# A top-k attention, SwiGLU and expert kernel: the last 64 keys' values padded with zeros to 128 rows, the queries transposed raw

## The chip, the cores and the metric

The kernel runs on one core of a Trainium2 chip. The metric is the device time of one execution in microseconds. The kernel before was timed three times: 1239.47, 1242.8 and 1243.44 us, so the median is 1242.8 us. The execution with the profile took 1240.91 us, of which the span from the first to the last instruction is 1239.3 us.

TensorE is PE in the profile (PEld is its weight load), VectorE is DVE, ScalarE is ACT, GpSimd is POOL, and SyncE, which only issues transfers here, is SP.

## The reference

Three layers follow each other. Only the first one is touched by the change.

```python
B, H, S, D = 4, 8, 576, 64                       # attention
scores = scale * np.matmul(q, k.transpose(0, 1, 3, 2))
kth = np.partition(scores, -32, axis=-1)[..., -32:-31]
scores = np.where(scores >= kth, scores, -1e9)   # keep the 32 largest of 576
attn = softmax(scores)
x = np.matmul(attn, v)                           # -> 2304 tokens x 512
...
xn = x / rms(x) * rms_g                          # SwiGLU, 512 -> 1536 -> 512
x = (silu(xn @ w_gate) * (xn @ w_val)) @ w_out
...
e_idx = argmax(x @ w_gate2 + bias[modality])     # one of 8 experts per token
out[t] = gate[t] * (relu(x[t] @ w1[e]) @ w2[e])
```

## The kernel before

**Tiles and steps.** For each batch and head there are 576 queries and 576 keys, that is 4 chunks of 128 and a rest of 64. A tile is 128 queries against all 576 keys. `tiles` lists 144 of them; two tiles make one of 72 steps. A main step has one chunk `c` of the two heads of a pair `p` (in batch 2, for the first two chunks, two chunks of one head). A remainder step has two tiles, each with the 64 last queries of head 0 above the 64 last queries of head 1 of one pair.

**One tile's way through the engines.** `dma_q` loads a step's queries six steps ahead. `split_q` (POOL, four steps ahead) makes two halves of them, `hi` (rounded to the short fp32r form) and `lo = q - hi`, each written twice side by side. `trans_q` (two steps ahead) transposes the four 128x128 blocks on PE (L465), and ACT copies the result to `qS` (L473, L478). `qk` multiplies them with the keys (L530). ACT copies the scores out (L543), and DVE finds the 32nd largest score of each row: two folded halves (L545 to L547), then four MAX8 and three MATCH_REPLACE8 for each tile (L565, L568), eight MAX8 on L565 for a step. ACT and POOL then make the softmax (L595, L599, L603), `tr` transposes it on PE (L625, L630) into `pT` (four chunks of keys) and `pr` (the last 64 keys; those of a step's even tile stand on partitions 0 to 63, those of the odd tile on 64 to 127). `av` multiplies both with the values (L671): per chunk of keys three products of fp16 halves, so 12 matmuls with 128 rows from `pT` and 3 with 64 rows from `pr`. `dma_v` loads the last 64 values twice, to both halves of the partitions, so that either half of `pr` finds them. Batch 0, heads 0 to 3, is done in fp32 instead of fp16 halves (`whole`).

**The second layer inside the first.** When the heads of one or two blocks of 128 tokens are done, they form a granule, and its SwiGLU (L729 to L750 on PE, u on L772, router logits on L809) is put into the attention steps in small atoms with a budget for each seventh of a step (`mlp_slot`). What is left after step 71 runs alone. The experts follow (L1161 to L1243).

**What sets the order.** The code is written in the order of `step`, but each engine's list of instructions is put in order by a scheduler before the launch, which goes by its own estimate of when operands are there. The order is fixed then: an engine runs its list from first to last and waits where an operand is late.

**Start.** `w_out` comes in twelve transfers on SP's queue into space of the other weights and is turned from float64 to fp16 halves by DVE (L279, L284, L288), ACT and POOL (L297); the first keys and queries are loaded between them.

Of the kernel before, what the change touches and what calls it, by code (L numbers as in the profile page):

```python
# [8 lines left out]
F32 = mybir.dt.float32  # L9
# [11 lines left out]
def topk_attention_swiglu_moe_kernel(  # L21
# [50 lines left out]

    NMB = B * CM
# [4 lines left out]
    def main_steps(b, cs):  # L78
        for p in range(NP):
            if len(cs) == 2:  # L80
                for hh in range(2):
                    steps.append([(b, p, hh, c) for c in cs])
            else:
                steps.append([(b, p, hh, cs[0]) for hh in range(2)])
        granules.append((len(steps) - 1, [b * CM + c for c in cs]))

    def rem_steps(b):
        for p in range(0, NP, 2):
            steps.append([(b, p, None, None), (b, p + 1, None, None)])
        if b % 2:  # L90
            granules.append((len(steps) - 1, [NMB + b // 2]))

# [121 lines left out]
    def front(exact):  # L214
# [218 lines left out]

        def dma_q(s):
            qr = ap_.tile([128, 2, D], F32, name="qr", tag="qr", bufs=QB)
            t0, t1 = steps[s]
            b, p, hh, c = t0
            if hh is not None and t1[2] == hh:
                src = q[b, 2 * p + hh, 0:SM, :].rearrange("(p c) d -> p c d", c=CM)
                nc.sync.dma_start(out=qr, in_=src[:, c:c + 2, :])  # L440
            else:
                for t, (b, p, hh, c) in enumerate(steps[s]):
                    if hh is not None:
                        src = q[b, 2 * p + hh, 0:SM, :].rearrange("(p c) d -> p c d", c=CM)
                        nc.sync.dma_start(out=qr[:, t, :], in_=src[:, c, :])
                    else:
                        for i in range(2):
                            nc.sync.dma_start(out=qr[i * SR:(i + 1) * SR, t, :], in_=q[b, 2 * p + i, SM:S, :])
            raw["q", s] = qr

        def split_q(s):
            qr = raw.pop(("q", s))
            qs = ap_.tile([128, 2, 2, 2, D], F32R, name="qs", tag="qs", bufs=2)
            z = zero.unsqueeze(2).unsqueeze(3).to_broadcast([128, 2, 2, D])
            q2 = qr.unsqueeze(2).to_broadcast([128, 2, 2, D])
            nc.gpsimd.tensor_tensor(out=qs[:, :, 0], in0=q2, in1=z, op=OP.add)
            nc.gpsimd.tensor_tensor(out=qs[:, :, 1], in0=q2, in1=qs[:, :, 0].bitcast(F32), op=OP.subtract)
            raw["qs", s] = qs

        def trans_q(s):  # L460
            qs = raw.pop(("qs", s))
            pt = ps_m.tile([128, 512], F32R, name="pq", tag="sm")
            for t in range(2):
                for j in range(2):
                    nc.tensor.transpose(  # L465
                        pt[:, (2 * t + j) * 128:(2 * t + j + 1) * 128],
                        qs[:, t, j].rearrange("p a d -> p (a d)"),
                        identr,
                    )
            src = pt.bitcast(F32)  # L470
# [883 lines left out]
```

## Time and profile before

| | PE | DVE | ACT | POOL | granted PE clock | MAX8 of L565 |
|---|---|---|---|---|---|---|
| whole span, 1239.3 us | 1138.8 | 928.2 | 830.5 | 731.2 | 0.94 | 576 |
| 61 to 205 us | 102.06 | 143.96 | 115.85 | 100.93 | 0.65 | 104 |
| 237 to 281 us | 41.51 | 23.62 | 30.43 | 26.38 | 0.88 | 16 |
| 281 to 824 us | 537.45 | 524.87 | 451.95 | 416.84 | 1.00 | 408 |
| 824 to 905 us | 79.10 | 17.48 | 30.55 | 33.40 | 1.00 | 0 |

All numbers are of the profiled execution (1240.91 us, span 1239.3 us); engine columns are busy microseconds, the clock is a share of full speed (1.00 is 2.4 GHz, 0.50 is 1.2 GHz). Attention steps run from about 21 to 824 us. From 824 to 905 us the rest of the SwiGLU runs, from there on the experts. A matmul's busy time reaches to its modelled end, which lies some 0.2 us behind the moment at which the next one can start; what a matmul costs is therefore read from start to start.

### The profile page before, as it was taken

What the parts mean: (1) busy time and instruction counts of PE and PEld (TensorE: products, weight loads), DVE (VectorE), ACT (ScalarE), POOL (GpSimd) and SP (SyncE); (2) the same over time, 40 slices, a digit from 0 to 9 for tenths busy, and PEclk for the clock granted to TensorE, in tenths of its full rate; (3) what the DMA queues carried; (4) which work ended last, traced back from release to release, by engine and by line L of the source; (5) the groups of instructions that cost most, each with busy time, mean ns of one, the idle gap of its engine ahead of it and who ended that gap; (6) DMA issues with size and microseconds to landing.
All of it is one profiled execution on the core that took longest, in us unless ns stands there. A gap on an engine that the chain in (4) does not pass through costs nothing. (4 is left out here: it accounts for less than half of the span.)

```text
span 1239.3 us, 32187 instructions
## 1 busy us (share of the span) xinstructions
PE 1138.8 (92%) x12286; PEld 1039.9 (84%) x12286; DVE 928.2 (75%) x2886; ACT 830.5 (67%) x1757; POOL 731.2 (59%) x843
## 2 busy tenths in 40 slices
PE   6976677999999999999999999999997999999994
PEld 6965566888999989999998999999986898798883
DVE  8999999759999999998999999971125526244161
ACT  6868888777888888878888887873333435344260
POOL 7866766858767879867889676564434312222100
PEclk9865676989999999999999999999997999999997
DMA  8242312011000111000011000013006726354230
GB/s 295 51 129 82 100 44 82 13 45 39 21 17 9 32 41 47 24 13 15 17 38 40 28 17 2 11 32 124 11 19 193 247 70 230 128 173 149 66 113 20
DMA packets 69624, 87.54 MB, mean 71 GB/s; under 512 B 34626, under 2 KB 43974, under 8 KB 69448
## 3 DMA queue, kind: packets, MB, share of 16 engines
q1 hardware_dynamic: 62360, 67.86, 17.9%
q0 software_dynamic: 5424, 13.16, 3.3%
q10 hardware_dynamic: 1664, 4.19, 0.9%
q8 instruction: 107, 1.75, 0.6%
q14 instruction: 69, 0.57, 0.2%
HBM read 75.58 MB, written 10.92 MB: 70 GB/s over the span
## 5 line engine op out<-in xcount | busy, mean ns | idle before, releaser
L565 DVE MAX8 w<-w 128x8 f32<-128x296 f32 x576 | 251.9, 462 | 1.2
L599 POOL TENSOR_TENSOR s<-s,r 128x576 f32<-128x576 f32 x144 | 201.1, 1417 | 31.3 <-ACT r L595 31.1
L568 DVE MATCH_REPLACE8 w<-w 128x296 f32<-128x296 f32 x432 | 194.9, 455 | 0.0
L750 PE MATMUL pf<-xT,wg 128*128 128x128 f16 (+1 forms) x2448 | 172.0, 224 | 4.2 <-DVE T L879 2.6
L750 PE MATMUL pf<-xT,wv 128*128 128x128 f16 (+1 forms) x2448 | 167.7, 222 | 0.0
L750 PE MATMUL po<-wo,h 128*128 128x264 f16 (+1 forms) x1296 | 157.4, 275 | 0.9 <-ACT t L777 0.9
L530 PE MATMUL ps<-kS,qS 128*128 128x288 f32 x640 | 138.6, 346 | 20.7 <-DVE w L546 19.6
L750 PEld LDWEIGHTS <-wg 128*128 128x128 f16 x2448 | 148.3, 99 | 11.1 <-issue 4.9
L750 PEld LDWEIGHTS <-wv 128*128 128x128 f16 x2448 | 145.3, 98 | 4.3
L750 PEld LDWEIGHTS <-h 128*128 128x128 f16 x1296 | 122.0, 98 | 18.8 <-issue 1.4
L1137 DVE TENSOR_TENSOR wl<-wr,wh 128x1024 fp32r<-128x1024 f32 x64 | 76.7, 1220 | 66.1 <-ACT wh L1136 66.1
L530 PEld LDWEIGHTS ps<-kS,qS 128*128 128x128 f32 x640 | 104.0, 215 | 23.8 <-ACT r L595 14.9
L603 ACT ACTIVATE s<-s,mbs 128x576 f32<-128x576 f32 x144 | 113.3, 789 | 14.2 <-POOL s L599 13.9
L595 ACT ACTIVATE r<-s,mbs 128x576 f32<-128x576 f32 x144 | 105.0, 781 | 15.1 <-POOL mbs L586 15.0
L625 PE MATMUL pt<-identr,s 128*128 128x128 f32 x576 | 97.6, 300 | 16.9 <-ACT s L603 16.1
L543 ACT COPY s<-ps 128x576 f32<-128x576 f32 x144 | 93.1, 646 | 22.1 <-PE ps L530 21.5
L1243 POOL DMA_INDIRECT out_dram<-o,idx x23 | 23.2, 1010 | 138.0 <-ACT o L1242 106.9
L1184 PE MATMUL ph<-xh,wh 128*128 128x256 f32 x352 | 99.7, 287 | 1.0 <-PEq L1301 1.0
L1184 PE MATMUL ph<-xl,wh 128*128 128x256 f32 x352 | 98.5, 282 | 0.0
L1184 PE MATMUL ph<-xh,wl 128*128 128x256 f32 x352 | 97.1, 284 | 0.8 <-issue 0.8
L782 POOL TENSOR_TENSOR t<-u,t 128x512 f32<-128x512 f32 x54 | 69.6, 1289 | 47.9 <-ACT t L777 30.3
L671 PE MATMUL pt<-vs,pT 128*128 128x64 f16 (+1 forms) x1680 | 88.4, 198 | 8.7 <-POOL pT L639 6.7
(205 smaller groups left out, 2779.0 us busy)
## 6 DMA issues: line engine op xcount, KB each, us to landing
wr<-in_moe_w_dram SPq DMA_DIRECT2D x56, 512.0 KB
wst<-in_moe_w_gate_dram SPq DMA_DIRECT2D x24, 256.0 KB
wst<-in_moe_w_val_dram SPq DMA_DIRECT2D x24, 256.0 KB
kr<-in_k_dram SPq DMA_DIRECT2D x32, 128.0 KB
vt<-in_v_dram SPq DMA_DIRECT2D x32, 128.0 KB
x_d<-xo SPq DMA_DIRECT2D x16, 256.0 KB
wr<-in_moe_w_dram ACTq DMA_DIRECT2D x8, 512.0 KB
qr<-in_q_dram SPq DMA_DIRECT2D x112, 32.0 KB
```

Of the source, the lines that this page charges most:

```text
L530: nc.tensor.matmul(out=ps[:, a, 0:HS], lhsT=qS[i // 2][:, i % 2, j, o2:o2 + 128], rhs=kt[:, m, ks], start=(n == 0), stop=(n == len(ops) - 1),)
L543: nc.scalar.copy(out=s.rearrange("p (a k) -> p a k", a=2), in_=ps[:, :, 0:HS])
L565: steps.append(lambda: dve.max(lists[t][:, 8 * r:8 * r + 8], src[t] if r == 0 else dst[t]))
L568: steps.append(lambda: dve.match_replace(out=dst[t], in_to_replace=lists[t][:, 8 * r:8 * r + 8], in_values=src[t] if r == 0 else dst[t], i ...
L595: nc.scalar.activation(out=d["r"], in_=d["s"], func=AF.Relu, scale=-BIG, bias=d["mb"][:, 1:2])
L599: nc.gpsimd.tensor_tensor(out=d["s"], in0=d["s"], in1=d.pop("r"), op=OP.subtract)
L603: nc.scalar.activation(out=d["s"], in_=d["s"], func=AF.Exp, scale=SCALE, bias=d["mb"][:, 0:1], accum_out=d["rs"])
L625: nc.tensor.transpose(pt[:, c * 128:(c + 1) * 128], e[:, e0 + c * 128:e0 + (c + 1) * 128], ident)
L671: nc.tensor.matmul(out=av_[o:o + n], lhsT=l, rhs=r, start=(a == 0), stop=(a == len(ops) - 1))
L750: nc.tensor.matmul(out=out_, lhsT=l, rhs=r, start=(a == 0), stop=(a == len(ops) - 1))
L1137: nc.vector.tensor_tensor(out=lo, in0=w[0], in1=hi.bitcast(F32), op=OP.subtract)
L1184: nc.tensor.matmul(out=pt, lhsT=l[:, fs], rhs=r[:, kk, :], start=(n == 0), stop=(n == 3 * KD - 1))
```

## The change

1. The pairs of a step change: the two heads of a pair with the same chunk in every main step; in a remainder step, tile `hh` holds head `hh` of two neighbouring pairs.
2. `dma_v` loads the last 64 values of head 0 to partitions 0 to 63 and those of head 1 to 64 to 127, once each, and POOL writes zeros beside them. `av` multiplies all 128 rows of `pr` with them; the other tile's probabilities meet zeros. A remainder tile uses all 128 columns of its stationary operand, writes 128 output rows for each of its two heads side by side, and half of them are read.
3. `dma_q` loads each query row twice side by side (a source with a repeated dimension), four steps ahead instead of six. `split_q` is gone. `trans_q` transposes two fp32 blocks instead of four; ACT writes `hi` (L471 in the changed file) and a full copy `qf` (L472), and POOL subtracts (L473 there).

```diff
     def main_steps(b, cs):
         for p in range(NP):
-            if len(cs) == 2:
-                for hh in range(2):
-                    steps.append([(b, p, hh, c) for c in cs])
-            else:
-                steps.append([(b, p, hh, cs[0]) for hh in range(2)])
+            for c in cs:
+                steps.append([(b, p, hh, c) for hh in range(2)])
...
         def dma_v(b, p):
             for i in range(2):
+                nc.gpsimd.memset(vt[(1 - i) * SR:(2 - i) * SR, i, CM, :], 0.0)
                 nc.sync.dma_start(out=vt[:, i, 0:CM, :], in_=v[b, h, 0:SM, :].rearrange("(p c) d -> p c d", c=CM))
-                for j in range(2):
-                    nc.sync.dma_start(out=vt[j * SR:(j + 1) * SR, i, CM, :], in_=v[b, h, SM:S, :])
+                nc.sync.dma_start(out=vt[i * SR:(i + 1) * SR, i, CM, :], in_=v[b, h, SM:S, :])
...
         def dma_q(s):
-            qr = ap_.tile([128, 2, D], F32, name="qr", tag="qr", bufs=QB)
+            qr = ap_.tile([128, 2, 2, D], F32, name="qr", tag="qr", bufs=QB)
+            for t, (b, p, hh, c) in enumerate(steps[s]):
+                if hh is not None:
+                    src = q[b, 2 * p + hh, 0:SM, :].rearrange("(p c) d -> p c d", c=CM)[:, c, :]
+                    nc.sync.dma_start(out=qr[:, t], in_=src.unsqueeze(1).to_broadcast([128, 2, D]))
...
-        def split_q(s):
-            nc.gpsimd.tensor_tensor(out=qs[:, :, 0], in0=q2, in1=z, op=OP.add)
-            nc.gpsimd.tensor_tensor(out=qs[:, :, 1], in0=q2, in1=qs[:, :, 0].bitcast(F32), op=OP.subtract)
...
         def trans_q(s):
-            pt = ps_m.tile([128, 512], F32R, name="pq", tag="sm")
+            pt = ps_m.tile([128, 512], F32, name="pq", tag="sm")
             for t in range(2):
-                for j in range(2):
-                    nc.tensor.transpose(
+                nc.tensor.transpose(
+                    pt[:, t * 128:(t + 1) * 128], qr[:, t].rearrange("p a d -> p (a d)"), ident
+                )
...
+            def post():
+                qf = ap_.tile([128, 2, 128], F32, name="qf", tag="qf", bufs=2)
+                nc.scalar.copy(out=hi, in_=cut(src))
+                nc.scalar.copy(out=qf, in_=src)
+                nc.gpsimd.tensor_tensor(out=lo, in0=cut(qf), in1=hi.bitcast(F32), op=OP.subtract)
...
-                at(s - 6, lambda s=s: dma_q(s))
+                at(s - 4, lambda s=s: dma_q(s))
...
-            at(s - 4, lambda s=s: split_q(s))
             at(s - 2, lambda s=s: trans_q(s))
...
         def av(i):
-            r0 = i % 2 * SR
-            parts = [(0, 128, hh)] if hh is not None else [(0, 64, 0), (64, 64, 1)]
+            parts = [(0, 128, p, hh)] if hh is not None else [(64 * m, 64, p + m, c) for m in range(2)]
...
-                    ks = slice(0, 128) if c2 < CM else slice(r0, r0 + SR)
-                    src, q0 = (pT, c2 * 128 + o) if c2 < CM else (pr, o)
-                    e = [src[ks, a, q0:q0 + n] for a in range(nh)]
+                    e = [pT[:, a, c2 * 128:(c2 + 1) * 128] if c2 < CM else pr[:, a] for a in range(nh)]
```

**SP's queue at the start.** Before, the queries of step 0 (`qr`, two transfers) are issued after two of the `w_out` transfers (`wg_108` to `wv_111`), those of step 1 after six, and those of steps 2 to 4 after all twelve:

```order
L266 DMA wg_108<-in_moe_w_out_dram 128x1024 x2
L375 DMA kr<-in_k_dram 128x256
L378 DMA kr<-in_k_dram 64x64
L375 DMA kr<-in_k_dram 128x256
L378 DMA kr<-in_k_dram 64x64
L445 DMA qr<-in_q_dram 128x64 x2
L266 DMA wg_108<-in_moe_w_out_dram 128x1024
L266 DMA wg_109<-in_moe_w_out_dram 128x1024 x3
```

Now the queries of steps 0 to 2 are the first ones, and they stand behind all twelve:

```order
L264 DMA wv_110<-in_moe_w_out_dram 128x1024 x3
L264 DMA wv_111<-in_moe_w_out_dram 128x1024
L373 DMA kr<-in_k_dram 128x256
L376 DMA kr<-in_k_dram 64x64
L373 DMA kr<-in_k_dram 128x256
L376 DMA kr<-in_k_dram 64x64
L264 DMA wv_111<-in_moe_w_out_dram 128x1024 x2
L441 DMA qr<-in_q_dram 128x2x64 x6
```

The first queries have moved from third place in the queue to its end.

**DVE's list at the start.** Before, the first scores (L545 to L547) stand behind 20 instructions on `w_out`, and 16 more of those are spread between the first searches:

```order
L284 SCALAR_TENSOR_TENSOR wp<-wv_110,wp 128x512
L545 TENSOR_TENSOR w<-s,ps 128x288
L546 TENSOR_TENSOR w<-s,ps 128x288
L288 SCALAR_TENSOR_TENSOR wp<-wv_110,wp 128x512
L547 MAX w<-w 128x8
L279 TENSOR_SCALAR wp<-wv_110 128x512
L565 MAX w<-w 128x8
```

Now all 36 stand ahead of them:

```order
L282 SCALAR_TENSOR_TENSOR wp<-wv_111,wp 128x512
L286 SCALAR_TENSOR_TENSOR wp<-wv_111,wp 128x512
L541 TENSOR_TENSOR w<-s,ps 128x288
L542 TENSOR_TENSOR w<-s,ps 128x288
L543 MAX w<-w 128x8
L561 MAX w<-w 128x8
```

**DVE's list at the end of the attention.** Before, the router's logits of the 14th block of tokens (L809) stand just ahead of the last MAX8 of step 71, and the check of the margins (L951) follows:

```order
L565 MAX w<-w 128x8
L809 SCALAR_TENSOR_TENSOR L<-po,mbias 128x8
L568 MATCH_REPLACE w<-w 128x296
L842 TENSOR_REDUCE mx<-L 128x1
L847 TENSOR_TENSOR d<-L 128x8
L565 MAX w<-w 128x8
L843 TENSOR_TENSOR T<-L,mx 128x8
```

Now the same instruction (L805 in the changed file) stands 17 MAX8 of line L561 ahead of the end of step 71, among new scores (L541, L542):

```order
L561 MAX w<-w 128x8
L541 TENSOR_TENSOR w<-s,ps 128x288
L542 TENSOR_TENSOR w<-s,ps 128x288
L564 MATCH_REPLACE w<-w 128x296
L805 SCALAR_TENSOR_TENSOR L<-po,mbias 128x8
L543 MAX w<-w 128x8
```

The SwiGLU has moved forward by about two steps against the attention. On PE, 1358 matmuls of the SwiGLU (L729 and L750) stand behind the last attention matmul before, and 1219 now.

## Rows read from the trace of the kernel before

**Rows 1.** The page: busy times, and the granted clock in 40 slices.

```profile
PE 1138.8 (92%) x12286; PEld 1039.9 (84%) x12286; DVE 928.2 (75%) x2886; ACT 830.5 (67%) x1757; POOL 731.2 (59%) x843
...
PEclk9865676989999999999999999999997999999997
```

**Rows 2.** Busy by stretch; columns: stretch, length, PE, PEld, DVE, ACT, POOL, clock, DMA.

```profile
61.00:205.00 144.00, 102.06 (x689) 88.46 (x685) 143.96 (x484) 115.85 (x246) 100.93 (x119) 0.65 0.31 88
237.00:281.00 44.00, 41.51 (x465) 36.19 (x462) 23.62 (x81) 30.43 (x73) 26.38 (x31) 0.88 0.12 33
281.00:824.00 543.00, 537.45 (x7241) 496.97 (x7240) 524.87 (x1790) 451.95 (x1011) 416.84 (x486) 1.00 0.09 24
824.00:905.00 81.00, 79.10 (x1223) 75.55 (x1221) 17.48 (x85) 30.55 (x64) 33.40 (x33) 1.00 0.19 60
```

**Rows 3.** Line L565 alone by stretch: DVE busy and count, clock, DMA.

```profile
281.00:824.00 543.00, 177.23 (x408) 1.00 0.09 24
```

**Rows 4.** Groups by line and shape, DVE, two of one shape: count, busy, mean.

```profile
L882 DVE TENSOR_TENSOR T<-T,O 128x8 f32<-128x8 f32 x16 | 9.3, 582 | 0.1
...
L844 DVE TENSOR_TENSOR T<-T,iota 128x8 f32<-128x8 f32 x16 | 2.5, 159 | 0.0
```

**Rows 5.** PE in order of time, 805 to 806 us; columns: start, length, instruction, count.

```profile
804.54 0.72 PE L671 MATMUL pt<-vs,pT 128*128 128x64 f16 x19
805.19 0.20 PE L671 MATMUL pt<-vs,pr 64*128 64x64 f16 x1
805.32 0.20 PE L671 MATMUL pt<-vs,pT 128*128 128x64 f16 x1
805.46 0.20 PE L671 MATMUL pt<-vs,pr 64*128 64x64 f16 x1
805.59 0.23 PE L671 MATMUL pt<-vs,pT 128*128 128x64 f16 x2
805.75 0.23 PE L671 MATMUL pt<-vs,pr 64*128 64x64 f16 x2
805.91 0.51 PE L750 MATMUL pf<-xT,wg 128*128 128x128 f16 x6
```

**Rows 6.** PE in order of time, 407 to 409 us.

```profile
407.44 0.54 PE L465 MATMUL pq<-identr,qs 128*128 128x128 f32 x4
407.82 0.40 PE L750 MATMUL pf<-xT,wv 128*128 128x128 f16 x4
...
408.11 0.64 PE L625 MATMUL pt<-identr,s 128*128 128x128 f32 x4
408.58 0.51 PE L671 MATMUL pt<-vs,pT 128*128 128x64 f16 x12
```

**Rows 7.** Groups by line and shape: count, busy us, mean ns, idle before.

```profile
L457 POOL TENSOR_TENSOR qs<-qr,qs 128x256 fp32r<-128x256 f32 x72 | 52.7, 732 | 2.3
...
L456 POOL TENSOR_TENSOR qs<-qr,zero 128x256 fp32r<-128x256 f32 x72 | 45.2, 627 | 32.7 <-PE pq L465 32.3 <-DMA qr<-in_q_dram 0.2
...
L473 ACT CAST qS<-pq 128x512 fp32r<-128x512 f32 x64 | 39.1, 611 | 1.5 <-PE pq L465 1.4
...
L814 ACT ACTIVATE xo<-po 128x256 f32<-128x256 f32 x36 | 13.9, 389 | 27.0 <-DVE L L809 21.0 <-PE po L750 6.0
```

**Rows 8.** Line L750 alone by stretch: PE and PEld busy with counts, clock, DMA.

```profile
824.00:905.00 81.00, 74.87 (x1132) 71.33 (x1132) 1.00 0.19 60
```

**Rows 9.** The start in order of time: SP, DVE and POOL.

```profile
16.92 4.40 SPq L445 DMA_DIRECT2D qr<-in_q_dram  x6
...
18.23 0.69 DVE L284 SCALAR_TENSOR_TENSOR wp<-wv,wp 128x512 int32<-128x512 int32 x1
18.82 0.45 DVE L545 TENSOR_TENSOR w<-s,ps 128x288 f32<-128x288 f32 x1
...
24.01 0.61 POOL L456 TENSOR_TENSOR qs<-qr,zero 128x256 fp32r<-128x256 f32 x1 [0.20 <-DMA qr<-in_q_dram]
```

**Rows 10.** Busy by stretch, columns as in the second group.

```profile
250.00:260.00 10.00, 8.37 (x68) 6.79 (x66) 4.68 (x22) 8.92 (x28) 5.27 (x8) 0.90 0.18 58
260.00:270.00 10.00, 9.79 (x87) 8.82 (x87) 6.44 (x19) 7.97 (x19) 5.67 (x6) 0.59 0.17 44
```

More of the change, by code (lines that the diff above doesn't have):

```diff
@@ L88, in rem_steps @@
         for p in range(0, NP, 2):
-            steps.append([(b, p, None, None), (b, p + 1, None, None)])
+            steps.append([(b, p, None, hh) for hh in range(2)])
         if b % 2:
@@ L434, in dma_q @@
         def dma_q(s):
-            qr = ap_.tile([128, 2, D], F32, name="qr", tag="qr", bufs=QB)
[L436 to L448, printed above, removed]
+            qr = ap_.tile([128, 2, 2, D], F32, name="qr", tag="qr", bufs=QB)
@@ new lines, in dma_q @@
+            for t, (b, p, hh, c) in enumerate(steps[s]):
+                if hh is not None:
+                    src = q[b, 2 * p + hh, 0:SM, :].rearrange("(p c) d -> p c d", c=CM)[:, c, :]
+                    nc.sync.dma_start(out=qr[:, t], in_=src.unsqueeze(1).to_broadcast([128, 2, D]))
+                else:
+                    for i in range(2):
+                        src = q[b, 2 * (p + i) + c, SM:S, :]
+                        nc.sync.dma_start(
+                            out=qr[i * SR:(i + 1) * SR, t], in_=src.unsqueeze(1).to_broadcast([SR, 2, D])
+                        )
@@ L449, in dma_q, with trans_q @@
             raw["q", s] = qr
-        def split_q(s):
+        def trans_q(s):
             qr = raw.pop(("q", s))
-            qs = ap_.tile([128, 2, 2, 2, D], F32R, name="qs", tag="qs", bufs=2)
-            z = zero.unsqueeze(2).unsqueeze(3).to_broadcast([128, 2, 2, D])
-            q2 = qr.unsqueeze(2).to_broadcast([128, 2, 2, D])
-            nc.gpsimd.tensor_tensor(out=qs[:, :, 0], in0=q2, in1=z, op=OP.add)
-            nc.gpsimd.tensor_tensor(out=qs[:, :, 1], in0=q2, in1=qs[:, :, 0].bitcast(F32), op=OP.subtract)
-            raw["qs", s] = qs
@@ L471, in trans_q @@
+            for t in range(2):
+                nc.tensor.transpose(
+                    pt[:, t * 128:(t + 1) * 128], qr[:, t].rearrange("p a d -> p (a d)"), ident
+                )
+            src = pt[:, 0:256].rearrange("p (t r) -> p t r", t=2)
             if steps[s][0][2] is not None:
                 dst = qS[s] = ap_.tile([128, 2, 2, 128], F32R, name="qS", tag="qS", bufs=2)
-                return lambda: nc.scalar.copy(out=dst, in_=src.rearrange("p (i j r) -> p i j r", i=2, j=2))
-            dst = qS[s] = ap_.tile([128, 2, 2, 192], F32R, name="qS", tag="qS", bufs=2)
@@ L476, in trans_q @@
-            nc.gpsimd.memset(dst[:, :, :, 64:128].bitcast(F32), 0.0)
-            heads = dst.rearrange("p t j (i r) -> p (t j) i r", i=3)[:, :, 0::2]
-            return lambda: nc.scalar.copy(out=heads, in_=src.rearrange("p (a i r) -> p a i r", a=4, i=2))
+                hi, lo, cut = dst[:, :, 0], dst[:, :, 1], lambda x: x
+            else:
+                dst = qS[s] = ap_.tile([128, 2, 2, 192], F32R, name="qS", tag="qS", bufs=2)
+                nc.gpsimd.memset(dst[:, :, :, 64:128].bitcast(F32), 0.0)
+                heads = dst.rearrange("p t j (i r) -> p t j i r", i=3)
+                hi, lo = heads[:, :, 0, 0::2], heads[:, :, 1, 0::2]
+                cut = lambda x: x.rearrange("p t (i r) -> p t i r", i=2)
@@ L499, in front @@
                 if KQ and s == 0:
-                    at(s - 6, lambda s=s: dma_q(s))
+                    at(s - 4, lambda s=s: dma_q(s))
                 at(s - 5, lambda b=b, p=p: split_k(b, p))
@@ L527, in qk @@
                 ks = slice(o, o + HS)
-                ops = [(o2, m, j) for o2, m in ([(0, hh)] if hh is not None else [(0, 0), (64, 1)]) for j in range(2)]
-                for n, (o2, m, j) in enumerate(ops):
+                ks_ = [(0, kS[b, p][:, hh, ks])] if hh is not None else [(64 * m, kS[b, p + m][:, c, ks]) for m in range(2)]
+                ops = [(o2, kt, j) for o2, kt in ks_ for j in range(2)]
+                for n, (o2, kt, j) in enumerate(ops):
                     nc.tensor.matmul(
-                        out=ps[:, a, 0:HS], lhsT=qS[i // 2][:, i % 2, j, o2:o2 + 128], rhs=kt[:, m, ks],
+                        out=ps[:, a, 0:HS], lhsT=qS[i // 2][:, i % 2, j, o2:o2 + 128], rhs=kt,
                         start=(n == 0), stop=(n == len(ops) - 1),
@@ L677, in post @@
             def post():
-                for o, n, h2 in parts:
-                    hd = 2 * p + h2
+                for m, (o, n, p2, h2) in enumerate(parts):
+                    hd = 2 * p2 + h2
                     nc.scalar.activation(
-                        out=x[x0:x0 + n, hd * D:(hd + 1) * D], in_=av_[o:o + n], func=AF.Copy,
+                        out=x[x0:x0 + n, hd * D:(hd + 1) * D], in_=d["pt"][o:o + n, m * D:(m + 1) * D], func=AF.Copy,
                         scale=d["rs"][o:o + n],
```

23 lines of the change are left out of this document (9 added, 14 removed).

## Prediction

> **What bounds the kernel now.** I read the page first: PE is busy 92% of the span, DVE 75%, and the granted clock is at half speed in many of the slices up to the ninth and full from then on [rows 1]. An average over stages decides nothing, so the busy time by stretch comes next [rows 2]. From 61 to 205 us DVE is busy 143.96 of 144 us and PE 102: the search for the top 32 and the conversion of weights set the pace. From 237 to 281 us DVE is busy only 23.6 of 44 us and PE 41.5, at a clock of 0.88: PE sets the pace. From 281 to 824 us PE is busy 537 of 543 us and DVE 525, at full clock: both are nearly full. From 824 to 905 us PE is busy 79 of 81 us and DVE 17: PE alone. So time can be won on PE in three stretches, and in the longest one DVE stands right behind it. That stretch holds 408 MAX8 of L565 [rows 3], eight for a step, so 51 steps of 10.65 us.
>
> How far DVE could go is less sure than its 525 us look. Two DVE instructions of one shape, 128x8, have means of 582 and 159 ns [rows 4], so a recorded duration can hold waiting.
>
> **The 64-row matmuls.** What a `pr` matmul costs is read from start to start. Nineteen `pT` matmuls, and the change to `pr`, take from 804.54 to 805.19, 0.65 us; a single `pr` 0.13 us; a single `pT` between two `pr` 0.14; two `pT` 0.16 and two `pr` 0.16 [rows 5]. So one more of a kind costs 0.03 us, the last one before a change 0.13, whichever kind it is: a change between 128 and 64 rows costs 0.10 us, each way. Every change has the same price, which waits for data would not have. The Trainium skill (TensorEngine Tiling (Array Packing), Key Properties) says that changing the tiling mode drains TensorE; the trace agrees, with these 0.10 us. The same list says that tiles on different rows work in parallel, and by that rule the padding gives up an overlap of at most 0.03 us for each of 177 pairs of `pr` matmuls, 5 us of the saving below. The trace shows none of it: the second of two `pr` matmuls costs the same 0.03 us as one more `pT` [rows 5].
>
> After the change every `av` matmul has 128 rows and columns. Their number stays 15 for a tile or a remainder head, since half of a 64-row matmul's array was idle and a 128-row one costs the 0.03 us of a `pT`. In PE's list of before, the 354 `pr` matmuls behind the scores of step 21 stand in 161 groups, since the order scatters some. At 0.20 us for both changes that is 32 us; 118 groups of three would give 24. I take 32 for the stretch from 281 to 824 us, nearly all of these 51 steps.
>
> **The query transposes.** Four fp32r ones take from 407.44 to 407.82, 0.38 us; four of raw fp32 (L625) from 408.11 to 408.58, 0.47 us [rows 6], so two cost 0.23. PE saves 0.15 us a step, 7 us in 51 steps. Together PE loses about 39 us of work in this stretch (bounds 24 + 7 = 31 and 39).
>
> **POOL and ACT.** POOL loses 72 additions of 627 ns and keeps 72 subtractions like L457's (732 ns) [rows 7]: 45 us less. The 32 memsets of 64x64 are not in the trace; between nothing and L456's 0.63 us each, at most 20 us, hidden on a POOL that is busy 417 of 543 us [rows 2]. On ACT one copy of 611 ns becomes two of half the size; L814 of that size takes 389 ns [rows 7], so +0.17 us a step, 9 us in a stretch where ACT has 91 us free. But the subtraction now lies between transposition and scores, behind POOL's queue. Its cover is the step between `trans_q` (two steps ahead) and `qk` (one ahead), 10.65 us; without it each late score would stop DVE. I cost it at nothing.
>
> **The loads.** The number of SP issues for a main step's queries stays two; six took 4.40 us [rows 9]. The doubled rows are not in the trace. They lie between nothing and the 7.1 us from the issue at 16.92 to the first use at 24.01 [rows 9], which is with all twelve `w_out` transfers ahead, and there are two steps, 21 us, between issue and use. Nothing, in the long stretch.
>
> **The start.** Here the cover is gone: the first queries now stand behind all twelve `w_out` transfers. In the trace the queries at that place reach POOL at 24.01, and the first scores reach DVE at 18.82 [rows 9]; with transposes, copies, subtraction and scores behind 24 us I expect these at about 29, 10 us later. DVE's list now has 16 more instructions on `w_out` ahead of them, at 0.59 us from start to start (18.23 to 18.82 [rows 9]) 9.4 us of other work. So the loss is between nothing and 10 us; with the cover as long as the delay, but ACT and PE not used to it, I take 3.
>
> **The tail.** The order has 1219 SwiGLU matmuls behind the attention instead of 1358. The trace records 1132 on L750 in those 81 us [rows 8], 0.072 us each, so 139 fewer save 10 us there, and put 10 us onto PE ahead of it.
>
> **The sum.** From 281 to 824 us PE has 39 - 10 = 29 us less to do, but DVE only 18 us of idle time to give up (543 - 524.9 [rows 2]). DVE did get to 100% from 61 to 205 us, with PE at 71%; here PE would still be at 97% ((537 - 29) / (543 - 18)), and each will wait for the other at times. I take 12 us, two thirds. From 237 to 281 us PE has some three steps' saving, 2 us. In all -12 - 10 - 2 + 3 = -21 us against the profiled execution: 1240.9 (span 1239.3 and 1.6 around it) - 21 = 1219.9. The median of the runs is 1.9 above that execution, so I forecast 1222.
>
> **Rivals.**
> DVE is the bound already, or PE's 0.10 us are waits that come back elsewhere: the long stretch keeps its 543 us and only the tail and the start count, -10 + 3 = -7, 1236. For it: DVE at 97% in that stretch. Against it: PE at 99%, and steps in which PE is the later of the two.
>
> DVE's durations hold much waiting and give way as PE does: PE's saving comes in whole, -29 - 10 - 2 + 3 = -38, 1205 (to 1202 with no loss at the start). For it: the 582 ns of L882 [rows 4]. Against it: POOL and ACT also have their queues.
>
> The slower side: the clock. PE's list gets thinner while DVE keeps its pace. Where PE was busy 8.37 of 10 us the granted clock was 0.90, and in the next 10 us 0.59 [rows 10]; at 0.88 as from 237 to 281 us, PE's remaining 537 - 29 = 508 us of the long stretch would take 577, 34 us more than before. With tail and start that is 34 - 10 - 2 + 3 = +25, 1268. It decides once the mean clock there is under 508/543 = 0.94. The Trainium skill (TensorE: Matmul & The Clock Gate, Part 1) says that the throttled state is the default and activity releases it; the trace agrees as far as the clock in rows 10 fell behind a gap. Against it: PE would still be near 97% busy, and it is at full clock from 281 us on.
>
> A late first score is the same side's smaller case: 10 us at the start with DVE full until 205 us, none of it caught by DVE's idle 20 us before 281, and 1229 instead of 1222.
>
> **Chances.** Forecast 53%, with 1211 to 1232 as its own range (the late start in it); only the tail 20%; PE's saving in whole 18%; the clock 8%; 1% for the rest. The range of 8 in 10 leaves out the clock and about half of the fastest case: 1204 to 1241. A measurement of this kernel tells 0.3% (3.7 us) from no change. Faster than 1239.1: the forecast, the fastest case and most of the second, 0.87. Within 0.3%: the upper end of the second, 0.05. Slower: 0.08.
>
> **What would show it.** Right: the L671 rows with one number of rows, back to back at 0.03 us; two transposes a step on the `pq` tile; DVE at 98% or more in the stretch after 281 us; 51 steps there in about 531 us; about 71 us between the last step and the experts' start. Wrong: a granted clock under 1.00 in the long stretch, DVE waiting on ACT's score copies behind a late POOL subtraction, a first score later than 32 us, or PE still at 99% with the same 543 us.

## The result and the profile after

The changed kernel takes 1224.5 us (median of 4 runs, 1222.1 to 1227.8), the kernel before 1241.1 beside it: ratio 0.987 [0.984, 0.990]. The forecast was 1222. The profiled execution, the fastest of the four, has a span of 1220.5 us, against 1239.3.

The busy times and the granted clock on the page of the changed kernel answer to [rows 1]:

```profile
PE 1087.4 (89%) x12142; PEld 1004.8 (82%) x12142; DVE 935.0 (77%) x2886; ACT 830.0 (68%) x1829; POOL 696.5 (57%) x803
...
PEclk9876676989999999999999999999998999999997
```

PE lost 51 us of busy time, POOL 35, and DVE gained 7. The busy times by stretch answer to [rows 2]; each stretch lies about where the same steps now lie:

```profile
69.00:214.00 145.00, 92.76 (x636) 82.06 (x637) 144.07 (x482) 115.65 (x254) 93.60 (x105) 0.67 0.31 88
256.00:292.00 36.00, 33.30 (x450) 31.64 (x451) 26.01 (x74) 26.89 (x64) 26.91 (x34) 0.95 0.18 48
292.00:818.00 526.00, 507.12 (x7195) 477.99 (x7192) 523.73 (x1790) 447.26 (x1051) 389.01 (x451) 1.00 0.11 29
818.00:907.00 89.00, 87.40 (x1278) 82.91 (x1276) 20.71 (x97) 31.59 (x67) 37.38 (x36) 1.00 0.17 58
```

In the long stretch PE and DVE have changed places: PE is busy 507 of 526 us, DVE 523.7, at full clock. Where that stretch begins and ends is read from DVE's search line, as in [rows 3]: eight MAX8 a step, the 169th opens step 21, the 576th is the last. These two, in DVE's order of time, before the change and after it:

```profile
281.20 0.47 DVE L565 MAX8 w<-w 128x8 f32<-128x296 f32 x1
...
820.02 0.47 DVE L565 MAX8 w<-w 128x8 f32<-128x296 f32 x1
```

```profile
291.64 0.45 DVE L561 MAX8 w<-w 128x8 f32<-128x296 f32 x1
...
816.62 0.47 DVE L561 MAX8 w<-w 128x8 f32<-128x296 f32 x1
```

The busy times between these two, before and after:

```profile
281.20:820.00 538.80, 533.25 (x7179) 493.01 (x7179) 521.91 (x1773) 447.75 (x997) 414.21 (x480) 1.00 0.09 23
```

```profile
291.60:816.60 525.00, 506.12 (x7171) 476.98 (x7172) 522.87 (x1788) 447.06 (x1050) 388.37 (x450) 1.00 0.11 29
```

So the span falls into three parts, and the experiments below use the same three, in us:

```
                      to step 21   step 21 to last MAX8   from there to the end    span
before                     281.2                  538.8                   419.3   1239.3
changed kernel             291.6                  525.0                   403.9   1220.5
difference                 +10.4                  -13.8                   -15.4    -18.8
```

The stretch from 818 to 907 us is not the counterpart of 824 to 905 in [rows 2]. Before the change the SwiGLU runs on to 926 us, 21 us behind the end of that stretch; the experts begin behind these groups, the last ones of the SwiGLU before and after:

```profile
925.31 1.36 PE L750 MATMUL po<-wo,h 128*128 128x256 f16 x11
```

```profile
906.46 1.36 PE L746 MATMUL po<-wo,h 128*128 128x256 f16 x11
```

From the last MAX8 to the last SwiGLU matmul it is 106.4 us before and 90.9 now. That is all of the 15.4 us: what follows takes 313 us in both.

A piece of PE's list with the last values' matmuls, columns as in [rows 5]:

```profile
401.15 0.57 PE L665 MATMUL pt<-vs,pT 128*128 128x64 f16 x14
401.56 0.22 PE L665 MATMUL pt<-vs,pr 128*128 128x64 f16 x2
401.62 1.28 PE L746 MATMUL pf<-xT,wv 128*128 128x128 f16 x20
...
403.45 0.44 PE L665 MATMUL pt<-vs,pT 128*128 128x64 f16 x9
403.72 0.19 PE L665 MATMUL pt<-vs,pr 128*128 128x64 f16 x1
403.75 0.19 PE L665 MATMUL pt<-vs,pT 128*128 128x64 f16 x1
403.78 0.25 PE L665 MATMUL pt<-vs,pr 128*128 128x64 f16 x3
403.87 0.33 PE L746 MATMUL pf<-xT,wv 128*128 128x128 f16 x3
```

From start to start every `pr` matmul now costs 0.03 us, wherever it stands; the 0.13 of [rows 5] is gone. The queries' two raw transposes answer to [rows 6]: 0.22 us, where four took 0.38.

```profile
418.13 0.38 PE L454 MATMUL pq<-identr,qr 128*128 128x128 f32 x2
418.35 2.13 PE L746 MATMUL po<-wo,h 128*128 128x256 f16 x18
```

By line and shape, the copies, the subtraction and the memsets answer to [rows 7]:

```profile
L473 POOL TENSOR_TENSOR qS<-qf,qS 128x256 fp32r<-128x256 f32 x72 | 53.4, 742 | 24.0 <-ACT qf L472 20.7 <-issue 1.9 <-PE pf L746 0.6
...
L472 ACT COPY qf<-pq 128x256 f32<-128x256 f32 x72 | 29.4, 408 | 0.0
L471 ACT CAST qS<-pq 128x256 fp32r<-128x256 f32 x72 | 28.5, 396 | 1.1 <-PE pq L454 1.1
...
L386 POOL MEMSET vt<- 64x64 f32 x32 | 4.7, 146 | 1.7
```

The search line of the long stretch alone, and the SwiGLU line of the last one, as in [rows 3] and [rows 8]; the second is one more way to see that a SwiGLU matmul still costs 0.07 us:

```profile
292.00:818.00 526.00, 177.68 (x408) 1.00 0.11 29
```

```profile
818.00:907.00 89.00, 84.25 (x1206) 79.28 (x1204) 1.00 0.17 58
```

And the start, as in [rows 9]: DVE's last conversion, and the first scores after a wait of 1.20 us.

```profile
27.69 0.69 DVE L286 SCALAR_TENSOR_TENSOR wp<-wv,wp 128x512 int32<-128x512 int32 x1
29.58 0.46 DVE L541 TENSOR_TENSOR w<-s,ps 128x288 f32<-128x288 f32 x1 [1.20 <-ACT s L539]
```

### The profile page after: what moved, and what is told of

It reads as the page before. It is cut to its first block, busy times and chain, and to the rows that moved or that the text cites. A ratio compares the mean times of both kernels' runs of the same rounds, so it can differ in the third digit from the quotient of the medians.

```text
span 1220.5 us, 31927 instructions
## 1 busy us (share of the span) xinstructions
PE 1087.4 (89%) x12142; PEld 1004.8 (82%) x12142; DVE 935.0 (77%) x2886; ACT 830.0 (68%) x1829; POOL 696.5 (57%) x803
## 5 line engine op out<-in xcount | busy, mean ns | idle before, releaser
L561 DVE MAX8 w<-w 128x8 f32<-128x296 f32 x576 | 251.4, 455 | 1.4
L746 PE MATMUL pf<-xT,wg 128*128 128x128 f16 (+1 forms) x2448 | 166.8, 222 | 7.2 <-DVE T L875 4.0
L746 PEld LDWEIGHTS <-wv 128*128 128x128 f16 x2448 | 149.2, 98 | 6.4 <-issue 1.7
L539 ACT COPY s<-ps 128x576 f32<-128x576 f32 x144 | 94.0, 652 | 19.8 <-PE ps L526 18.8
L665 PE MATMUL pt<-vs,pT 128*128 128x64 f16 x1680 | 79.9, 196 | 14.2 <-POOL pT L635 8.2
```

The source lines that it names most:

```text
L539: nc.scalar.copy(out=s.rearrange("p (a k) -> p a k", a=2), in_=ps[:, :, 0:HS])
L561: steps.append(lambda: dve.max(lists[t][:, 8 * r:8 * r + 8], src[t] if r == 0 else dst[t]))
L665: nc.tensor.matmul(out=d["pt"][:, m * D:(m + 1) * D], lhsT=l, rhs=r, start=(a == 0), stop=(a == len(ops) - 1))
L746: nc.tensor.matmul(out=out_, lhsT=l, rhs=r, start=(a == 0), stop=(a == len(ops) - 1))
```

## The experiments

Each ratio is to the kernel before, run beside it on the same chip. Nearly every edit changes the fixed order of the whole program, and that alone moves times; how far is a question that the experiments had to settle. In the table the three parts are those of above, from one profiled execution of each kernel; the executions of one kernel differ by 3 to 10 us in all, so a part that differs by a few us tells nothing by itself.

```
                                        ratio [95% interval]     to step 21   to last MAX8   to the end
values only (e1_v_only)                 0.988 [0.987, 0.990]          290.4          531.9        405.1
queries only (e2_q_only)                1.012 [1.010, 1.014]          283.9          561.5        408.6
changed, first queries earlier (e3)     0.993 [0.990, 0.995]          298.4          529.0        402.5
changed, more transposes (e4)           0.999 [0.998, 1.000]          288.0          535.6        417.3
changed, less on VectorE (e5)           0.992 [0.990, 0.994]          295.2          532.0        406.7
before, less on VectorE (e6)            1.008 [1.006, 1.010]          279.2          543.7        424.0
changed, 64-row matmuls (e7)            1.005 [1.003, 1.008]          303.6          542.1        404.2
queries only, turned first (e8)         1.007 [1.004, 1.009]          278.2          554.1        419.0
changed, turned first (e9)              0.994 [0.992, 0.996]          290.1          533.9        405.9
changed, more on VectorE (e10)          0.980 [0.977, 0.982]          291.5          523.5        398.0
changed, most on VectorE (e11)          0.986 [0.984, 0.988]          293.6          535.4        394.6
before, more on VectorE (e12)           1.004 [1.002, 1.006]          283.5          559.3        404.0
```

**The price of the 64 rows, in one order.** The changed kernel, but the last values' matmul takes only the 64 rows with values:

```diff
-    e = [pT[:, a, c2 * 128:(c2 + 1) * 128] if c2 < CM else pr[:, a] for a in range(nh)]
+    e = [pT[:, a, c2 * 128:(c2 + 1) * 128] if c2 < CM else pr[i % 2 * SR:i % 2 * SR + SR, a] for a in range(nh)]
-    w = [vt[:, a, h2, c2, :] for a in range(nh)]
+    w = [vt[(slice(0, 128) if c2 < CM else slice(i % 2 * SR, i % 2 * SR + SR)), a, h2, c2, :] for a in range(nh)]
```

> The changed kernel, but the matmul of the last values takes only the 64 rows that hold values, as before the change; the zeros are still written and loaded beside, and every engine's order of instructions is that of the changed kernel, word for word. So it is the price of the changes between 64- and 128-row matmuls alone. Theory 1 (each change costs 0.10 us on TensorE, and TensorE's time counts about fully, as it did for the two more transposes a step): the stretch from step 21 to the last MAX8 grows from 525 by 20 to 32 us, the total by 25 to 38, ratio to the kernel before 1.007 to 1.018. Theory 2 (the prediction's: VectorE hides much of it, of 32 us about 12 count in the long stretch, and little of the tail): 1.000 to 1.006 less the tail's 10, so 0.995 to 1.000. Theory 3 (the switch is no cost, the gain came from another order): 0.984 to 0.989.

1250.1 us, against 1224.5: 23 us by the two ratios, 29 by the spans (the profiled execution is the slowest of its six). By the ratio that lies just below theory 1's range, into which the interval reaches, and clear above those of theories 2 and 3; the long stretch grew by 17.1 us, short of theory 1's 20. So the switch has its price, and in the long stretch TensorE's time counts by more than half. The whole gain hangs on it: all the rest of the change, with the 64-row matmuls kept, is 0.5% slower than the kernel before. Since every engine's list is the same, this pair is the cleanest comparison here. The same piece of PE's list as above, in this kernel:

```profile
418.04 0.57 PE L665 MATMUL pt<-vs,pT 128*128 128x64 f16 x14
418.54 0.23 PE L665 MATMUL pt<-vs,pr 64*128 64x64 f16 x2
...
418.70 1.29 PE L746 MATMUL pf<-xT,wv 128*128 128x128 f16 x20
...
420.42 0.44 PE L665 MATMUL pt<-vs,pT 128*128 128x64 f16 x9
420.79 0.20 PE L665 MATMUL pt<-vs,pr 64*128 64x64 f16 x1
420.93 0.20 PE L665 MATMUL pt<-vs,pT 128*128 128x64 f16 x1
421.06 0.26 PE L665 MATMUL pt<-vs,pr 64*128 64x64 f16 x3
421.25 1.68 PE L746 MATMUL pf<-xT,wv 128*128 128x128 f16 x27
```

The same 16 matmuls take 0.66 us (418.04 to 418.70) instead of 0.47, the same 14 take 0.83 instead of 0.42: 0.19 us for one group of `pr`, 0.41 for two. So it is throughout: from the matmul ahead of a group of `pr` to the one behind it, the 167 groups of the long stretch take 0.20 us more in the median, and 28 us in sum. By stretch:

```profile
69.00:214.00 145.00, 98.85 (x608) 84.89 (x609) 139.59 (x466) 111.73 (x245) 90.36 (x103) 0.61 0.31 90
256.00:304.00 48.00, 43.35 (x521) 38.85 (x518) 30.50 (x89) 34.97 (x87) 29.72 (x40) 0.89 0.15 42
304.00:846.00 542.00, 534.39 (x7151) 494.09 (x7147) 523.76 (x1788) 447.99 (x1047) 385.73 (x448) 1.00 0.11 28
```

In the long stretch PE has 27 us more to do (534.4 against 507.1) and the stretch is 17.1 us longer: 0.6 us for each us of PE. Behind the last MAX8 it is the same within 0.3 us. Before step 21 it is 12.0 us longer, at a lower granted clock (0.61 against 0.67 in the stretch from 69 us, 0.89 against 0.95 in the next). Only 47 groups of `pr` stand there, some 9 us of PE at the 0.20 of the long stretch, an estimate. So at that price the switches do not make up the 12 us even if all of it counts. The clock and the difference between two executions are left for the rest, and one execution of each kernel does not tell them apart.

**The two halves of the change.** The values' half alone, against the changed kernel, with the old path of the queries, and the queries' half alone, with the old loads, matmuls and steps of the values:

```diff
values only:
-    qr = ap_.tile([128, 2, 2, D], F32, name="qr", tag="qr", bufs=QB)
+    qr = ap_.tile([128, 2, D], F32, name="qr", tag="qr", bufs=QB)
...
+    nc.gpsimd.tensor_tensor(out=qs[:, :, 0], in0=q2, in1=z, op=OP.add)
+    nc.gpsimd.tensor_tensor(out=qs[:, :, 1], in0=q2, in1=qs[:, :, 0].bitcast(F32), op=OP.subtract)
...
queries only:
-    nc.gpsimd.memset(vt[(1 - i) * SR:(2 - i) * SR, i, CM, :], 0.0)
-    nc.sync.dma_start(out=vt[i * SR:(i + 1) * SR, i, CM, :], in_=v[b, h, SM:S, :])
+    for j in range(2):
+        nc.sync.dma_start(out=vt[j * SR:(j + 1) * SR, i, CM, :], in_=v[b, h, SM:S, :])
```

> The changed kernel with the old way of the queries (loaded once, six steps ahead, split on POOL, four fp32r transposes); only the pairs of a step and the 128-row values with zeros are changed. In the order 1136 SwiGLU matmuls stand behind the last attention matmul (1316 before, 1135 in the changed kernel). Theory (the changes between 64 and 128 rows are nearly all of PE's saving): about 32 of the 39 us of PE work go, the tail is 12 to 13 us shorter, the start is as before, steps 21 to 71 take 516 to 522 us instead of 532; in all 20 to 25 us under the kernel before, ratio 0.980 to 0.984. Rival (the gain comes from POOL's 45 us less and the shorter way of the queries): no more than the tail's 12 us, ratio 0.990 or above.

> The kernel before with only the queries changed (doubled rows four steps ahead, two raw transposes, halves behind them); values and pairs of a step as before. 1160 SwiGLU matmuls stand behind the last attention matmul. Theory: PE saves 7 us in steps 21 to 71, the first scores come 10 us later and cost 3 us at the start, the tail is 11 us shorter, and the long stretch stays within 3 us of 532 us, or grows, since PE has more SwiGLU to do in it; in all 4 to 10 us under the kernel before, ratio 0.992 to 0.997. Rival (POOL's 45 us are what counts): 15 us or more, ratio 0.988 or under.

Both missed. The values alone gave 14.7 us of gain by the ratio, between the two ranges: the tail shrank by 14.2 us, but step 21 came 9.2 us later than before, where the start was expected to be as before. The queries alone made the kernel slower by 14.6 us, which neither text had. Adding the queries' half on top of the values' half changes little (0.988 to 0.987). The halves don't add up. In the queries-only kernel the long stretch reads:

```profile
284.00:845.00 561.00, 545.04 (x7260) 500.63 (x7261) 536.22 (x1790) 454.37 (x1060) 392.15 (x440) 1.00 0.11 29
```

PE is busy 545 us there, 12 more than before (533 of 538.8), though its transposes are cheaper: its order puts 174 more SwiGLU matmuls into the stretch, and the last part is 10.7 us shorter. These two nearly cancel, so the loss is PE's idle time in the stretch, 16 us instead of 5.6, and 2.7 us before step 21. On POOL the subtraction waits, by the waits of that stretch (us in total, times, longest):

```profile
POOL qS L471 <- ACT qf L470: 20.6, 11, 4.8
```

That is the wait that the prediction cost at nothing. But none of PE's own waits there names `qS`; its score matmuls wait 2.5 us, for DVE to free their buffer. DVE waits 10.7 us for ACT's copies of the scores, against 5.8 before.

**Is it this wait?** The queries turned first among a step's preparations instead of last, in the queries-only kernel and in the changed one:

```diff
-    at(s - 2, lambda s=s: trans_q(s))
+    prep.setdefault(s - 2, []).insert(0, lambda s=s: trans_q(s))
```

> The queries' change alone, with the turning of a step's queries put first among that step's preparations instead of last, so that the copies on ScalarE and the subtraction on GpSimd have some 1 to 4 us more before the scores need them. Theory 1 (the wait of the scores for this longer chain made the queries' change alone 13 us slower): half or more of the loss goes, ratio 0.995 to 1.006. Theory 2 (it was the other fixed order of the work, not this wait): ratio stays at 1.007 to 1.018.

> The changed kernel with the turning of a step's queries put first among that step's preparations instead of last. Theory 1 (the scores' wait for the copies on ScalarE and the subtraction on GpSimd still costs in the changed kernel): the stretch from step 21 to the last MAX8 falls from 525 by 4 to 10 us and the start by up to 10 (the first scores on VectorE come no later than 32), ratio to the kernel before 0.974 to 0.984. Theory 2 (TensorE has slack now and hides it; the order is merely another one): within 4 us of the changed kernel, ratio 0.984 to 0.990.

The first won 0.5% back: 1.007 lies at the edge between the two ranges, and its interval reaches into both. PE's idle time in the long stretch fell from 16 to 10 us and POOL's wait from 20.6 to 14.2, but the order changed as well: 1316 SwiGLU matmuls stand behind the attention instead of 1160. The second was slower than the changed kernel by 0.7%, which no theory had. So this wait is not shown to be the cause of the queries-only kernel's loss, nor is it ruled out.

**The start.** The first three steps' queries loaded six steps ahead, as before the change:

```diff
-    at(s - 4, lambda s=s: dma_q(s))
+    at(s - (6 if s < 3 else 4), lambda s=s: dma_q(s))
```

> The changed kernel with the queries of steps 0 to 2 loaded six steps ahead again, so that they stand between the first weights as before; later ones four steps ahead. Theory (the late first queries cost 3 us on a DVE that is full up to 205 us): 3 us under the changed kernel, ratio to the kernel before about 0.984, first scores on DVE at about 19 us instead of 29.6. Rival (the DVE idles some 20 us between 232 and 292 us anyway, so a late start is caught up there): the same time as the changed kernel, 0.9867.

Both missed. The first search started at 22.0 us instead of 30.8, but by step 3 it stood at 69.3, where the changed kernel stands as well, and by step 18 at 255.6 against 232.1. The order had 369 SwiGLU matmuls ahead of that step, the changed kernel 217. The early start won nothing here: it was caught up by step 3, and what the order did later is larger.

**More work for PE.** Two more transposes a step into the half of `pq` that nothing reads:

```diff
-    for t in range(2):
-        nc.tensor.transpose(pt[:, t * 128:(t + 1) * 128], qr[:, t]..., ident)
+    for t in (2, 3, 0, 1):
+        nc.tensor.transpose(pt[:, t * 128:(t + 1) * 128], qr[:, t % 2]..., ident)
```

> The changed kernel with two more transposes in each step, of the same queries into a part of the PSUM tile that nobody reads: 0.23 us of PE work a step, 12 us in steps 21 to 71. The order puts 1264 instead of 1135 SwiGLU matmuls behind the attention, which by itself lengthens the tail by 9 us. Theory (DVE is the bound in steps 21 to 71 now): these steps stay within 3 us of the 515 us of the changed kernel, in all 7 to 11 us more than the changed kernel. Rival (PE is still the bound there): 12 us on top of the tail's 9, steps 21 to 71 at 525 us or more, in all 18 us or more above the changed kernel.

144 transposes at 0.11 us are 16 us; the kernel took 16.5 us longer (1240.9; 15 by the two ratios), about as much. The long stretch grew by 10.6 us, more than the theory allowed, and the total stayed below the rival's 18:

```profile
288.00:823.60 535.60, 511.21 (x7091) 479.58 (x7089) 527.01 (x1778) 446.10 (x1049) 386.16 (x448) 0.99 0.11 28
```

But this does not show that the transposes lengthened that stretch. The order took 184 SwiGLU matmuls out of it (4178 instead of 4362), 13 us at 0.072 us each, about as much as the added transposes put in (102 at 0.11 us, 11 us). PE's busy time rose by 5 us; DVE's records fill 98% of the stretch. The added work came out at the end, in the last part, which is 13.4 us longer. Why the stretch grew as well is open; the order is another one.

**Less, and more, on VectorE.** `PL1` says of which tiles from 36 on the `pT` subtraction is done by a copy on ScalarE and a subtraction on GpSimd instead of on VectorE: of every fourth in both kernels.

```diff
-        PL0, PL1 = 36, 4
+        PL0, PL1 = 36, 2        # more with 8, most with 1000
```

> The changed kernel with the subtraction for pT taken off VectorE for 27 more tiles from tile 36 on (a copy on ScalarE and a subtraction on GpSimd in its place): about 16 us less on VectorE, 16 more on ScalarE, 31 more on GpSimd. Theory 1 (VectorE alone bounds the long stretch after the change, 523.7 of 526 us busy): the stretch from step 21 to the last MAX8 falls from 525 to 511 to 515, ratio to the kernel before 0.975 to 0.979. Theory 2 (the engines bound it together, and any work on one of them that is not waited for costs elsewhere): it stays within 5 us of 525, ratio 0.983 to 0.991. Theory 3 (GpSimd, already waited for by the scores through the queries' second halves, is late now): over 530, ratio above 0.991.

> The same relief of VectorE, in the kernel before the change. Theory 1 (TensorE bounds it before, 528 of 534 us busy): no gain, ratio 0.996 to 1.004, the stretch from step 21 to the last MAX8 stays at 536 to 541 us. Theory 2 (bound together): 0.989 to 0.996, 531 to 536 us.

Both were slower than without this edit, the changed kernel by 0.5%. The changed one's numbers are those of theory 3, but its mechanism does not show: GpSimd is busy only 415 of the 532 us, its subtraction of the queries waits 6.3 us there instead of 13.8, and DVE waits for the scores' copies 0.5 us in all. For the kernel before no theory had a loss. The subtraction's group in the long stretch, of the changed kernel, and then of it with the edit; the busy times with the edit stand below:

```profile
L637 DVE TENSOR_TENSOR pT<-pt,pT 128x512 f16<-128x512 f32 x76 | 51.0, 673 | 0.1
```

```profile
L637 DVE TENSOR_TENSOR pT<-pt,pT 128x512 f16<-128x512 f32 x51 | 34.5, 675 | 0.3 <-ACT pT L631 0.3
```

```profile
295.00:827.00 532.00, 508.64 (x7142) 477.39 (x7142) 524.20 (x1764) 456.47 (x1074) 415.00 (x475) 1.00 0.11 29
```

25 subtractions, 16.5 us of records, are gone from DVE, and its busy time is the same, 524 us. So those 524 are not work alone. In the order of time after the change each record of DVE ends after the next has begun:

```profile
501.55 0.45 DVE L564 MATCH_REPLACE8 w<-w 128x296 f32<-128x296 f32 x1
501.92 0.07 DVE L564 MATCH_VALUE_LOAD w<-w 128x8 f32 x1
501.98 0.45 DVE L564 MATCH_REPLACE8 w<-w 128x296 f32<-128x296 f32 x1
502.35 0.67 DVE L637 TENSOR_TENSOR pT<-pt,pT 128x512 f16<-128x512 f32 x1
502.95 0.45 DVE L561 MAX8 w<-w 128x8 f32<-128x296 f32 x1
```

A MATCH_REPLACE8 takes 0.37 us from start to start, its record 0.45: 0.07 to 0.08 us of each of the longer records lie over the next one (0.01 us of the short MATCH_VALUE_LOAD), and a gap shorter than that is not seen. The Trainium skill (Perfetto Trace Analysis, Optimizing Scalar/DVE Operations) says that a profiled latency holds a write acknowledgement that overlaps with the next instruction; the trace agrees as far as the overlap of 0.08 us goes, and what fills it no run here shows. Taking the lower quartile of the start-to-start times of each group as its work, an estimate, DVE has about 494 us of work in the 538.8 before, 495 in the changed kernel's 525 and 478 in the 532 with this edit (512, 511 and 502 by the median). The work did fall by the 25 subtractions, and the busy time did not show it.

The other direction:

> The opposite of the relief of VectorE: in the changed kernel 13 more tiles from tile 36 on have their pT subtraction on VectorE instead of ScalarE and GpSimd (about 9 us more on VectorE, 8 less on ScalarE, 15 less on GpSimd). Theory 1 (VectorE bounds the long stretch): it grows from 525 to 531 to 535 us, ratio to the kernel before 0.991 to 0.996. Theory 2 (the chain over ScalarE and GpSimd is what costs, as the relief's loss of 7 us suggests): it falls to 519 to 524, ratio 0.980 to 0.986.

> The changed kernel with every pT subtraction from tile 36 on on VectorE (with 13 more tiles the stretch from step 21 to the last MAX8 had been 523.5 us, against 525.0). Theory 1 (VectorE's share of work, about 18 us more than in the changed kernel, now ends last): the stretch grows to 528 to 540 us, ratio to the kernel before 0.982 to 0.995. Theory 2 (the chain over ScalarE and GpSimd still ends last): 518 to 525 us, ratio 0.970 to 0.980.

> The kernel before the change with 13 more tiles' pT subtraction on VectorE, as in the faster version of the changed kernel. Theory 1 (before the change TensorE holds the long stretch, 533 of 539 us busy, so what VectorE and GpSimd share matters little): ratio to the kernel before 0.995 to 1.003. Theory 2 (the same gain as there, 7 to 9 us, for the shorter chain and the SwiGLU matmuls that the order then puts into the attention): 0.990 to 0.994.

With half of those subtractions back on VectorE the changed kernel takes 1215.6 us (1214.2 to 1219.6): it beats both kernels, and is the fastest of all here. The long stretch lies in the range of theory 2, the ratio at its edge. Its order puts 90 SwiGLU matmuls more into that stretch and as many fewer behind it; the last part is 5.9 us shorter, and the stretch takes them in and still is 1.5 us shorter. Whether a shorter chain over ScalarE and GpSimd made the room, as theory 2 has it, is not shown; the order is another one. With all of them on VectorE, the stretch grows by 10.4 us, the range of theory 1, and the last part is 9.3 us shorter. But the order also put 131 more SwiGLU matmuls into the stretch than in the changed kernel, 9 us of PE, so VectorE is not shown to be what lengthened it:

```profile
293.00:829.00 536.00, 514.21 (x7297) 483.88 (x7295) 533.60 (x1814) 437.19 (x1025) 364.12 (x428) 1.00 0.11 29
```

The kernel before gains nothing by the same edit (1.004, a little beyond theory 1's range): its stretch grew by 20 us and its last part fell by 15. The order moved 218 SwiGLU matmuls into the stretch, 16 us at 0.072 each. That fits a kernel in which PE has no room for them, though here, too, the order is another one.

## Why the prediction came out

The sum was right within 3 us (1222 against 1224.5; from the profiled execution -21 against -18.8), and that was in part luck. Of its three parts, the long stretch and the tail were too small by 2 and 5 us, and the part ahead of step 21 was wrong by 9 us the other way; the errors cancel.

- **64-row matmuls.** The 0.10 us each way, read from [rows 5], held: 0.19 and 0.41 us for one and two groups in the same list of instructions. 32 us of PE's work in the long stretch were forecast, for 161 groups; in the identical order 28 came, for 167 groups at 0.20 us in the median (27 by the busy times).
- **How much of it shows.** The prediction capped the gain by DVE's 18 us of idle time and took two thirds, 12 us. The stretch gave 13.8. The way there was partly wrong. DVE's idle time before is not 18 us but, by the estimate above, some 27 to 45, since its records overlap; so the cap of 18 us was not there. The suspicion that a record can hold waiting fits: single records of L882 [rows 4] run from 157 to 1320 ns. And by the prediction's own prices PE lost 34 us of work there, not 29, since the order put 75 SwiGLU matmuls more into the stretch, 5 us, and not 139 and 10 us (PE's busy time fell by 27). In the identical order 0.6 of PE's saving counts. Without the switches PE is idle 19 us there instead of 8, and DVE waits for the scores' copies 0.2 us instead of 7.0: part of what PE saves becomes its own waiting.
- **Ahead of step 21.** Forecast +3 for the start and -2 from 237 to 281 us, measured +10.4. This is the term that failed. The start itself came as worked out (first scores at 29.58 us, forecast about 29). What was missed is the order. In the changed kernel 660 SwiGLU matmuls stand ahead of step 21, 137 more than before, 10 us at 0.072 us each [rows 8]; the prediction put the matmuls that leave the tail onto the long stretch. The experiments bear this out. The four kernels with 517 to 523 ahead (before, e2, e6, e12) reach step 21 at 279 to 284 us, and the late start of the queries alone is among them. The six with 660 and no switches (changed, e1, e5, e9, e10, e11) reach it at 290 to 295 us, and the values alone, which start as early as the kernel before (first search at 21.1 us), are among those. So the 10 us go with the order and not with the late queries. The switches taken away should have won some us here; the 64-row kernel has the same 660 ahead and reaches step 21 at 303.6.
- **The tail.** Forecast -10, measured -15.4 behind the last MAX8, of which in identical order nothing comes from the switches. The counts of 1358 and 1219 were taken some 40 matmuls too early in the list, at about the 2260th of its 2300 on L671; behind the last one stand 1316 before and 1135 after. Behind the last MAX8, from where the 15.4 us are measured, stand 1454 and 1242: 212 fewer, 15 us at 0.072 each. The 81 us that the prediction took for the tail end 21 us ahead of the last SwiGLU matmul. Its sign of about 71 us to the experts' start therefore did not come (90.9 us from the last MAX8), while the price per matmul held (106.4 us for 1454).
- **The queries.** Two raw transposes take 0.22 us, as forecast, and the ACT copies 408 + 396 ns instead of 611, near the forecast's +0.17. The memsets took 4.7 us in all, near the lower bound. "Cost at nothing" for the subtraction: POOL does wait in front of it in the changed kernel's long stretch:

```profile
POOL qS L473 <- ACT qf L472: 13.8, 10, 3.7
```

DVE, which a late score would stop, waits there for the scores' copies 0.2 us in all:

```profile
DVE w L541 <- ACT s L539: 0.2, 1, 0.2
```

So in the changed kernel the term held; yet the queries' half alone was 1.2% slower, and DVE waited 10.7 us for those copies there (5.8 before).

Of the rivals, "only the tail" fell by the long stretch, "PE's saving in whole" by the 0.6 that counts in the identical order, and the slower clock by the 1.00 of the long stretch. Two of the prediction's signs for it, DVE at 98% or more and 51 steps in about 531 us (527, when 12 is taken from the 538.8 between the two MAX8), came as 99.6% and 525. The first of them proves less than it seemed to, as the relief of VectorE shows.

What stays open is why the queries' half alone is slower. What its long stretch took over from the last part is given back there; what is left is 10 us of PE's idle time, for which no single wait answers. An order held fixed while only the queries' path changes was not tried, since this edit changes the instructions themselves. So the cause is shown for the values' half alone, which by itself is as fast as the whole change (0.988 against 0.987).

## What to carry to other kernels

Where short matmuls with fewer rows are scattered among full ones, read the cost of each change from start to start, and consider padding with zeros: a padded matmul cost no more than a short one here (0.03 us), each pair of changes 0.2 us. A busy share of 99% is not yet a bound: take work off that engine and see whether the share falls, and read its start-to-start times first. When an edit reorders the whole program, compare with an edit that leaves the order alone, since edits that only moved instructions were worth some 5 to 10 us in this kernel. Count what the order has moved from one part into another before a part's time is given a cause. After a change that frees one engine, share out the work between the others anew: it gave 0.7% here, and nothing in the kernel before.

## What the runs showed of the hardware

DVE's longer records overlap the next one by about 0.08 us, and its busy time stayed at 524 us with 25 subtractions taken away. The price of a change between 64 and 128 rows is about the same at both ends of a group, 0.20 us for both ends in the median of 167 groups, and `pr` matmuls of 64 rows gained nothing over 128 otherwise (0.03 us each in both). With the switches in the list, the granted clock of the early stretch was lower (0.61 against 0.67) in the same order of instructions; whether it fell because of the switches, because the work lay later, or from one execution to the next, no run here tells.
